# An output projection as seven block products instead of eight

## The chip, the cores and the metric

The kernel runs on one core of a Trainium2 chip. The metric is the time of one execution on the device in microseconds (us), lower is better. A core has TensorE (matmuls into PSUM, called PE in the profile; its weight loads are PEld), VectorE (DVE), ScalarE (ACT), GpSimd (POOL), and SyncE (SP), which here only issues DMAs. PSUM has eight banks of 128 x 512 float32 values; GpSimd does not read it in this kernel.

## What is computed

For 2048 tokens of width 640, with `xn = layernorm(x)`:

```python
# A: linear attention, 32 heads of 20, feature map = two softmaxes
qkv = xn @ wqkv
phi_q, phi_k = features(q, w_phi), features(k, w_phi)
o = (phi_q @ (phi_k.T @ v)) / (phi_q @ sum(phi_k) + 1e-6)
A = o.reshape(S, D) @ wo                  # 2048 x 640 by 640 x 640
# B: an MLP, 640 -> 1728 -> 640
h = gelu(layernorm(xn) @ w1 + b1)
B = h @ w2 + b2
return x + A + B
```

The change concerns the line with `wo`, the output projection.

## The kernel before

Everything is kept transposed: feature chunks of 128 (`KC` = 5 of them) on the partitions, tokens along the free dimension, in four blocks of 512 (`NB` = 4). A float32 operand is split into two parts, a high one (ScalarE copies the value to a shorter type) and a low one (the rest, a subtraction on VectorE or GpSimd; line 57). A product takes three matmuls: high by high, high by low, low by high (`mm3`, line 69).

The stages in order of time: layer norm and the first MLP groups for blocks 0 and 1; from about 217 to 443 us the key stage (the loop at line 1009: keys, queries, values and feature maps for 16 tiles of 128 tokens, four projections to a tile, and `kv_tile`, line 965); then the MLP for blocks 2 and 3 with the attention of all blocks beside it; from 643 us the output projection.

In the key stage only TensorE's order is written by hand; the other engines and the DMA queue are ordered by an automatic scheduler. At its tiles 1, 2, 3, 6 and 7 one chunk of `wo` each is loaded, split, and both parts are stored to DRAM (lines 1035 to 1044). From line 1350 on VectorE, ScalarE and GpSimd too work in program order; the DMAs on SP are still placed by the scheduler.

`Mlp.tick` (line 220) is called after each `mm3`. It counts ticks, runs the steps that are due (`after`, line 227) and advances a generator of side work (`beside`). So a due tick sets at which place of the program an operation enters its engine's queue; the engine runs it when its inputs are there.

MLP groups 1 to 5 for blocks 2 and 3 already use seven block products (`cross`, line 411). For group 6 the two blocks go one after the other (`passes`, line 286).

`Attention` collects a block's result in `ob`. `quotients` (line 1227) divides it by the denominators: five shuffles on VectorE (line 1255) and five multiplications on GpSimd (line 1257). Blocks 0 and 1 are stored to DRAM and come back through `load_ob` (line 1379); those of blocks 2 and 3 stay. The multiplications of block 3 fall into the output projection. `Attention.split` (line 1263) makes a block's two parts, a chunk at a time, while it reorders the tokens: the high part on ScalarE, the low one on VectorE. Then it loads the accumulator (input and MLP sum, `a_dram`) of blocks 0 and 1.

`load_wo` (line 1284) brings the split `wo` back. The projection itself (lines 1400 to 1417) runs over four blocks and five output chunks `m`; for each it sums five contraction chunks in one PSUM bank, with banks 6 and 7 in turn. VectorE adds the bank to the accumulator (line 1416) and SP stores the result (line 1417). The last output chunk is done in two halves of 256 tokens. Splits of blocks 1, 2 and 3 are put at steps 3, 28 and 53.

Of the kernel before, what the change touches and what calls it, by code (L numbers as in the profile page):

```python
# [8 lines left out]
F32 = mybir.dt.float32  # L9
F32R = mybir.dt.float32r  # L10
AF = mybir.ActivationFunctionType
ALU = mybir.AluOpType
# [3 lines left out]
P = 128  # L16
S, D, F, H, DH = 2048, 640, 1728, 32, 20
KC = D // P
NB = S // 512
# [27 lines left out]
def f(ap):  # L47
    return ap.bitcast(F32)
# [3 lines left out]
def tile_kernel(ctx: ExitStack, tc: tile.TileContext, x, xT, wkT, wqT, wv, wphi, wo, w1, b1, w2, b2,  # L52
                ident, mmask, emask, vsel, out):
    nc = tc.nc
    ctx.enter_context(nc.allow_low_precision(reason="float32 operands are split exactly into float32r parts"))

    def split(hi, lo, src, scale=None, eng=nc.vector, first=nc.scalar):

        if scale is None:
            if first is nc.scalar:  # L60
                nc.scalar.activation(hi, src, AF.Copy)  # L61
            else:
                first.tensor_copy(hi, src)
            eng.tensor_tensor(lo, src, f(hi), op=ALU.subtract)  # L64
        else:
            nc.scalar.activation(hi, src, AF.Copy, scale=scale)
            nc.vector.scalar_tensor_tensor(lo, src, scale, f(hi), op0=ALU.mult, op1=ALU.subtract)

    def mm3(ps, lh, ll, rh, rl, first, last, **kw):
        nc.tensor.matmul(ps, lh, rh, start=first, stop=False, **kw)  # L70
        nc.tensor.matmul(ps, lh, rl, start=False, stop=False, **kw)  # L71
        nc.tensor.matmul(ps, ll, rh, start=False, stop=last, **kw)  # L72
# [17 lines left out]
    wo_dram = [tc.dram_tile([P, KC, D], F32, name=f"wo{p}") for p in "hl"]  # L90
# [12 lines left out]
    banks = ctx.enter_context(tc.tile_pool(name="banks", bufs=1, space=PSUM))  # L103
# [110 lines left out]
    class Mlp:  # L214
        def __init__(self, slots, hid):
            self.hid, self.turn, self.slots, self.beside, self.raw = hid, 0, slots, iter(()), {}
            self.ph, self.px, self.po = Banks(0, 1, 2), Banks(3, 4), Banks(5, 6, 7)
            self.due, self.ticks = [], 0

        def tick(self):  # L220

# [5 lines left out]
        def after(self, ticks, step):  # L227

            if ticks:
                self.due.append((self.ticks + ticks, len(self.due) and self.due[-1][1] + 1, step))  # L230
                self.due.sort(key=lambda d: d[:2])
            else:
                step()
# [282 lines left out]
    def finish(p):  # L516
        for _ in p:
            pass
# [4 lines left out]
    x0 = load_x(range(2), xp)  # L523
# [42 lines left out]
    def step(gen, n):  # L566
        for _ in range(n):
            next(gen, None)
# [440 lines left out]
    for t, i in [(t, i) for t in range(14) for i in range(4)] + TAIL:  # L1009
        if (t, i) in ((4, 0), (8, 0)):  # L1010
            b = t // 4 + 1
            y[b] = [yp.tile([P, KC, 512], F32R, name=f"y{p}{b % 2}") for p in range(2)]
            for p in range(2):
                nc.sync.dma_start(f(y[b][p]), y_dram[b - 2][p])
        ps = proj(t, i)
        pq = 1 + t % 3
        if t and t % 4 == 0:
            store_phi(t // 4 - 1, i)
        if i == 0:
            evac = evacuate(ps, 0, 0)  # L1020
# [12 lines left out]
        if tk is not None:  # L1033
            kv_tile(tk, fts.pop(tk), vbuf[tk % 2])
        if i == 0 and t in (1, 2, 3, 6, 7):

            kc = (1, 2, 3, 6, 7).index(t)
            lo = rp.tile([P, D], F32, name="r1")
            hi = rp.tile([P, D], F32R, name="r2")
            nc.sync.dma_start(lo, wo[kc * P:(kc + 1) * P, :])  # L1040
            with tc.issue_after(evac):
                split(hi, lo.bitcast(F32R), lo, eng=nc.gpsimd)
            for w, wd in zip((f(hi), lo), wo_dram):
                nc.sync.dma_start(wd[:, kc, :], w)
        if (t, i) == (11, 0):
            mlp = Mlp((0, 3, 2, 1), ((1, 2), (0, 3)))
            mlp.ph = ptile
            mlp.fetch_pair(0, False)
        if (t, i) == (12, 3):
            with tc.issue_after(evac):  # L1050
                w1t, parts = mlp.take_pair(0, False, 0)
                for part in parts:
                    part()
            mlp.fetch_pair(0, True)
        if (t, i) == (15, 3):
            w2t, late = mlp.take_pair(0, True, 3)
            late.pop(0)()
# [96 lines left out]
    class Attention:  # L1154
# [105 lines left out]
                for i in range(3):  # L1260
                    yield

        def split(self, c, eng):

            b = self.b

            def tokens(ap):
                return ap.rearrange("p (q t n) -> p t q n", q=4, t=4)

            def parts(ap):  # L1270
                return ap.rearrange("p (t q n) -> p t q n", q=4, t=4)

            if c == 0:
                self.oh, self.ol = (yp.tile([P, KC, 512], F32R, name=f"y{p}{b % 2}") for p in range(2))
            if c < KC:
                nc.scalar.activation(parts(self.oh[:, c, :]), tokens(self.ob[:, c, :]), AF.Copy)
            if c:
                eng.tensor_tensor(parts(self.ol[:, c - 1, :]), tokens(self.ob[:, c - 1, :]), f(parts(self.oh[:, c - 1, :])), op=ALU.subtract)
            if c == KC and b < 2:

                acc[b] = tfp.tile([P, KC, 512], F32, name=f"tf{b}")
                nc.sync.dma_start(acc[b], a_dram[b])

    def load_wo():

        for p, wd in enumerate(wo_dram):
            w = wp.tile([P, 4, D], F32R, name=f"w{(2, 0)[p]}")
            nc.sync.dma_start(f(w), wd[:, 0:4, :])
            last = rp.tile([P, D], F32R, name=f"r{1 + p}")
            nc.sync.dma_start(f(last), wd[:, 4, :])  # L1290
            wol.append([w[:, kc, :] for kc in range(4)] + [last])

    def first_split():
        for c in range(KC + 1):
            at[0].split(c, nc.vector)
            if c % 2:
                yield

# [98 lines left out]
    finish(before)  # L1397
    load_ob(1)

    pw_ = Banks(6, 7)  # L1400
    step = 0
    for b in range(NB):
        oh, ol = at[b].oh, at[b].ol
        for m in range(KC):
            ms = slice(m * P, (m + 1) * P)

            for cols in [slice(0, 512)] if (b, m) != (NB - 1, KC - 1) else [slice(0, 256), slice(256, 512)]:
                pw = pw_()[:, cols]
                for c in range(KC):
                    mm3(pw, wol[0][c][:, ms], wol[1][c][:, ms], oh[:, c, cols], ol[:, c, cols], c == 0, c == KC - 1)  # L1410
                    step += 1
                    mlp.tick()
                    for n, at_ in enumerate((3, 28, 53), 1):
                        if step - at_ in range(KC + 1):
                            at[n].split(step - at_, nc.vector)
                nc.vector.tensor_tensor(acc[b][:, m, cols], pw, acc[b][:, m, cols], op=ALU.add)
                nc.sync.dma_start(out[ms, b * 512 + cols.start:b * 512 + cols.stop], acc[b][:, m, cols])
# [63 lines left out]
```

## Time and profile before

| | us |
|---|---|
| median of 3 runs (715.44 to 717.74) | 716.49 |
| the profiled execution | 716.96 |
| its span, first to last instruction | 715.2 |
| PE, DVE, ACT, POOL busy | 704.0, 513.1, 342.1, 421.7 |
| output projection, first matmul to last evacuation | 643.3 to 711.8 |

The profile is one execution. A row of a timeline has the start from the span's beginning, the duration, the engine, the line of the program, the operation and what it writes and reads; in brackets how long the engine was idle before it and what ended that. Several rows of one kind in a row are merged (x2, x3), and then the duration is that of all of them. A row of a table by stretch has the stretch, its length, the busy time and the count of each engine, the granted clock of TensorE, the share of the DMA engines and GB/s. A row of a line's instructions has the shortest, the median and the longest duration in ns.

### The profile page before, as it was taken

Reading aid. Unit: us, or ns where it says so; the run is one execution under the profiler, and the core shown is the slowest. Engines: PE = TensorE matmul, PEld = TensorE weight load, DVE = VectorE, ACT = ScalarE, POOL = GpSimd, SP = SyncE. Lnnn points to the kernel's source line nnn. Section 1 sums busy time; section 2 is a strip of 40 time slices with the busy share of each in tenths; the row PEclk is TensorE's granted clock in tenths of the full one; section 3 lists DMA queues with packets and bytes.
Section 4 is the critical chain, followed back from the end, with each engine's and each line's share of the span. In section 5 each row is a group of like instructions: output and inputs, shape, how many; then the busy total and the mean of one; then the engine's idle time right before and its main releaser. Section 6 shows DMA issues by size and latency. Waiting matters only on the chain.

```text
span 715.2 us, 9745 instructions
## 1 busy us (share of the span) xinstructions
PE 704.0 (98%) x3381; PEld 591.2 (83%) x3381; DVE 513.1 (72%) x820; ACT 342.1 (48%) x563; POOL 421.7 (59%) x360
## 2 busy tenths in 40 slices
PE   8989999999999999999999999999999999999998
PEld 6868888878878888888888888888888878888886
DVE  7776754978754788788888877747679785784632
ACT  6434453444433544554444547357666666560200
POOL 3521223657235998798787979548689887540400
PEclk9999999999999999999999999999999999999999
DMA  9813643474722226325500708864355568545222
GB/s 325 290 44 110 196 134 102 154 243 159 224 91 110 74 91 219 97 89 196 121 0 13 177 0 322 223 205 125 109 160 168 171 181 274 188 127 212 80 83 73
DMA packets 65767, 106.56 MB, mean 149 GB/s; under 512 B 7462, under 2 KB 31814, under 8 KB 63838
## 3 DMA queue, kind: packets, MB, share of 16 engines
q1 hardware_dynamic: 65414, 105.93, 46.5%
q8 instruction: 26, 0.43, 0.2%
q14 instruction: 23, 0.19, 0.1%
q10 hardware_dynamic: 304, 0.01, 0.0%
HBM read 71.37 MB, written 34.55 MB: 148 GB/s over the span
## 4 chain that ended last, share of the span: by engine, by line
PE 79%; DVE 7%; POOL 4%; DMA 4%; issue 3%; ACT 2%; SPq 1%; POOLq 0%; DVEq 0%; ACTq 0%
PE bank L898 23%; PE bank L70 16%; PE bank L72 15%; PE bank L71 15%; PE bank L968 2%; PE bank L696 2%; POOL m L933 2%; PE bank L1206 1%; PE bank L1207 1%; POOL w L64 1%; DMA t<-t 1%; DMA xq<-in_xT 1%; POOL m L944 1%; PE bank L323 1%; PE bank L324 1%
## 5 line engine op out<-in xcount | busy, mean ns | idle before, releaser
L898 PE MATMUL bank<-wkh,y 128*128 128x512 f32 (+1 forms) x480 | 139.5, 364 | 0.0
L70 PE MATMUL bank<-y,w 128*128 128x512 f32 (+1 forms) x294 | 114.4, 389 | 1.0 <-ACT m L283 1.0
L71 PE MATMUL bank<-y,w 128*128 128x512 f32 (+1 forms) x294 | 113.6, 387 | 0.0
L72 PE MATMUL bank<-y,w 128*128 128x512 f32 (+1 forms) x294 | 113.6, 386 | 0.0
L64 POOL TENSOR_TENSOR w<-r,w 128x640 fp32r<-128x640 f32 x32 | 52.2, 1645 | 98.8 <-ACT w L61 68.0
L70 PE MATMUL bank<-m,w 128*128 128x512 f32 x260 | 102.7, 395 | 3.5 <-DVE acc L328 3.2
L72 PE MATMUL bank<-m,w 128*128 128x512 f32 x260 | 101.3, 390 | 0.0
L71 PE MATMUL bank<-m,w 128*128 128x512 f32 x260 | 101.3, 389 | 0.0
L898 PEld LDWEIGHTS bank<-wkh,y 128*128 128x128 f32 x480 | 87.5, 188 | 13.3
L898 PE MATMUL bank<-wkl,y 128*128 128x512 f32 (+1 forms) x240 | 87.4, 364 | 0.0
L70 PEld LDWEIGHTS bank<-y,w 128*128 128x128 f32 x294 | 55.2, 188 | 12.8 <-ACT m L283 1.2
L72 PEld LDWEIGHTS bank<-y,w 128*128 128x128 f32 x294 | 55.2, 188 | 11.3
L71 PEld LDWEIGHTS bank<-y,w 128*128 128x128 f32 x294 | 55.2, 188 | 10.9
L934 ACT ACTIVATE m<-m,rs_all 128x1280 f32<-128x1280 f32 x32 | 43.7, 1365 | 42.9 <-POOL m L933 42.8
L70 PEld LDWEIGHTS bank<-m,w 128*128 128x128 f32 x260 | 48.8, 188 | 15.9 <-DVE acc L328 5.1
L936 DVE TENSOR_REDUCE sm<-m 128x64 f32<-128x1280 f32 x32 | 47.4, 1482 | 15.6 <-ACT m L934 15.4
L898 PE MATMUL bank<-w,y 128*128 128x512 f32 x240 | 57.4, 391 | 0.0
L72 PEld LDWEIGHTS bank<-m,w 128*128 128x128 f32 x260 | 48.8, 188 | 10.3
L71 PEld LDWEIGHTS bank<-m,w 128*128 128x128 f32 x260 | 48.8, 188 | 9.8 <-DVE m L458 0.2
L933 POOL TENSOR_TENSOR m<-m,mx 128x640 f32<-128x640 f32 (+2 forms) x48 | 44.4, 938 | 19.3 <-DVE mx L922 19.3
L328 DVE TENSOR_TENSOR acc<-bank,acc 128x512 f32<-128x512 f32 x70 | 46.9, 684 | 10.5 <-PE bank L72 5.4
L64 DVE TENSOR_TENSOR m<-m,m 128x512 fp32r<-128x512 f32 (+1 forms) x34 | 27.6, 819 | 35.5 <-ACT m L61 35.5
(182 smaller groups left out, 1461.6 us busy)
## 6 DMA issues: line engine op xcount, KB each, us to landing
r<-in_w SPq DMA_DIRECT2D x52, 320.0 KB
e<-e SPq DMA_DIRECT2D x40, 256.0 KB
e<-acc SPq DMA_DIRECT2D x52, 160.0 KB
acc<-in_xT SPq DMA_DIRECT2D x4, 1280.0 KB
t<-t SPq DMA_DIRECT2D x8, 512.0 KB
tf<-t SPq DMA_DIRECT2D x2, 1536.0 KB
xb<-in_x SPq DMA_DIRECT2D x8, 320.0 KB
xq<-in_xT SPq DMA_DIRECT2D x10, 256.0 KB
```

The lines of the kernel that those rows point to most:

```text
L64: eng.tensor_tensor(lo, src, f(hi), op=ALU.subtract)
L70: nc.tensor.matmul(ps, lh, rh, start=first, stop=False, **kw)
L71: nc.tensor.matmul(ps, lh, rl, start=False, stop=False, **kw)
L72: nc.tensor.matmul(ps, ll, rh, start=False, stop=last, **kw)
L323: nc.tensor.matmul(pw, w2h[:, ms], hh, start=False, stop=False)
L328: nc.vector.tensor_tensor(acc[b][:, m, :], pw, acc[b][:, m, :], op=ALU.add)
L696: nc.tensor.matmul(ps[:, u * nh * DF:(u + 1) * nh * DF], raw[:nh * DH, u * P:(u + 1) * P], wpt[:nh * DH, g, :nh, 1:], start=True, stop=True)
L898: nc.tensor.matmul(ps, lh[:, kc, c], rh[:, kc], start=n == 0, stop=n == 3 * KC - 1)
L933: subs[n, t] = nc.gpsimd.tensor_tensor(ep[:, s], a, b, op=ALU.subtract)
L934: exps[n, t] = nc.scalar.activation(e, e, AF.Exp, scale=rs_all[:, t:t + 1])
L936: nc.vector.tensor_reduce(sm, e.rearrange("p s (h f) -> p (s h) f", f=DH), axis=AX, op=ALU.add)
L968: nc.tensor.matmul(kvp[g // 2][:, (g % 2) * 240:(g % 2) * 240 + 240].rearrange("p (s f) -> p s f", s=4), v[:, g * VS:(g + 1) * VS], ft[:, ...
```

## The change

The projection is done by pairs of token blocks (0 and 1, then 2 and 3). For each contraction pair `q` (chunks 2q, 2q+1, of the first four) and each output pair `k` (output chunks 2k, 2k+1, of the first four) the product of two 2 x 2 arrangements of blocks takes seven block products in place of eight, in Winograd's form of Strassen's method. The weight side has the blocks a11, a12, a22 and the sums s1 to s4; the token side has b11, b21, b22 and the differences t1 to t4. Contraction chunk 4 is added by `rest`, output chunk 4 is done as before by `column`.

- In the key stage, at tiles 1 and 6, two chunks of `wo` are loaded, four sums are formed on GpSimd, and chunks and sums (128 x 768) are split and stored. Chunk 4 is done at tile 4.
- `load_wo` has three parts, into other buffers; the accumulators of blocks 0 and 1 go to weight buffers (`load_a`), and `load_ob(1)` is called earlier.
- The differences t1 to t4 are formed in place in `ob` on GpSimd (`combine`, 16 subtractions of 128 x 512) and split like plain blocks (`turn`). All of this is put at written ticks, counted from the projection's start.
- A product's bank is read as soon as its sum is needed and then added to further, so banks 0 to 5 are read several times.
- `after` numbers its steps with a counter of its own; steps due at one tick run in the order in which they were given, as before.

```diff
-        if i == 0 and t in (1, 2, 3, 6, 7):
...
+        if i == 0 and t == 4:
...
+        if i == 0 and t in (1, 6):
+            q = t // 6
+            raw = [rp.tile([P, D], F32, name=f"r{j}") for j in (1, 2)]
...
+            with tc.issue_after(evac):
+                for o, x0, x1, op in ((sm[:, 0], a21, a22, ALU.add), (a21, a11, a21, ALU.subtract),
+                                      (sm[:, 1], sm[:, 0], a11, ALU.subtract), (sm[:, 2], a12, sm[:, 1], ALU.subtract)):
+                    nc.gpsimd.tensor_tensor(o, x0, x1, op=op)
+                o = 0
+                for r, eng in (*zip(raw, 2 * [nc.gpsimd]), (sm.rearrange("p i k n -> p (i k n)"), nc.vector)):
+                    n = r.shape[1]
+                    split(h[:, o:o + n], r.bitcast(F32R), r, eng=eng)
+                    nc.sync.dma_start(wo_dram[1][:, q, o:o + n], r)
+                    o += n
+            nc.sync.dma_start(wo_dram[0][:, q], f(h))
...
+    def load_wo(n):
...
+        else:
+            wop[1][1] = mtile(0, F32R)
+            nc.sync.dma_start(f(wop[1][1]).rearrange("p r d -> p (r d)"), wo_dram[1][:, 1, :1280])
...
+        if b == 3:
+            load_a(0)
...
+            mlp.after(14, lambda: load_wo(0))
         else:
-            load_wo()
+            load_wo(1)
+            load_ob(1)
+            load_wo(2)
             mlp.beside = both(mlp.beside, first_split())
     finish(before)
-    load_ob(1)
+    load_a(1)
...
+    def combine(b0, i, q):
+        c0, c1 = 2 * q, 2 * q + 1
+        (co, bo), (cx, bx), (cy, by) = {1: ((c0, 0), (c0, 1), (c0, 0)), 3: ((c0, 1), (c1, 1), (c0, 1)),
+                                        2: ((c1, 1), (c1, 1), (c0, 0)), 4: ((c1, 0), (c1, 0), (c1, 1))}[i]
+        return lambda: nc.gpsimd.tensor_tensor(at[b0 + bo].ob[:, co], at[b0 + bx].ob[:, cx], at[b0 + by].ob[:, cy], op=ALU.subtract)
...
+    for c in range(KC):
+        steps += both_parts(2 * c, plain, 1, c)
+    for n, i in enumerate((1, 3, 2, 4)):
+        for q in range(2):
+            steps += [(3 + 4 * n + 2 * q, combine(0, i, q)), (38 + 4 * n + 2 * q + 2 * (n > 1), combine(2, i, q))]
+    for n, i in enumerate((1, 2, 4, 3)):
+        for q in range(2):
+            steps += both_parts(11 + 4 * n + 2 * q + (n > 0), turn, 0, i, q)
+            steps += both_parts(47 + 4 * n + 2 * q + 3 * (n > 0), turn, 2, i, q)
+    for n, c in enumerate(range(KC)):
+        steps += both_parts(28 + 2 * c, plain, 2, c)
+    for c, n in ((0, 37), (2, 39), (1, 45), (3, 47), (4, 49)):
+        steps += both_parts(n, plain, 3, c)
+    for tick, step in steps:
+        mlp.after(tick, step)
+
+    for b0 in (0, 2):
+        bank = [{n: banks.tile([P, 512], F32, name=f"bank{3 * k + i}") for i, n in enumerate("abc")} for k in range(2)]
+
+        def read(n, k, i, b, last=True):
+            o = acc[b0 + b][:, 2 * k + i]
+            nc.vector.tensor_tensor(o, bank[k][n], o, op=ALU.add)
...
+        for k in range(2):
+            product("a", k, "a11", "b11", True)
+            read("a", k, 0, 0, False)
+        for k in range(2):
+            product("c", k, "a12", "b21", True)
+            rest("c", k, 0, 0)
+            read("c", k, 0, 0)
+        column(b0, whole)
+        if b0 == 0:
+            column(1, whole)
...
+        for k in range(2):
+            product("a", k, "s3", "t3")
+            read("a", k, 1, 0)
+        for k in range(2):
+            product("b", k, "s4", "b22")
+            rest("b", k, 0, 1)
+            read("b", k, 0, 1)
+        for k in range(2):
+            rest("a", k, 1, 1)
+            read("a", k, 1, 1)
+        if b0 == 2:
+            column(3, halves)
```

`plain` splits a chunk of a block as it is. `both_parts` puts the high part (ScalarE) at the tick and the low part (VectorE) one tick later. The products left out here are s1 by t1 (bank b), s2 by t2 (bank a) and a22 by t4 (bank c, opened anew), in this order after the columns. A `product` has two steps, `q` = 0 and 1.

More of the change, by code (lines that the diff above doesn't have):

```diff
@@ L229, in after @@
             if ticks:
[L230 removed]
+                self.count += 1
+                self.due.append((self.ticks + ticks, self.count, step))
                 self.due.sort(key=lambda d: d[:2])
@@ L1261, in quotients, with split @@
                     yield
[L1263 to L1274, printed above, removed]
+        def split(self, c, part, hl=None):
+            src = self.ob[:, c].rearrange("p (q t n) -> p t q n", q=4, t=4)
+            hi, lo = (z.rearrange("p (t q n) -> p t q n", q=4, t=4) for z in hl or (self.oh[:, c], self.ol[:, c]))
+            if part == 0:
+                nc.scalar.activation(hi, src, AF.Copy)
+            else:
+                nc.vector.tensor_tensor(lo, src, f(hi), op=ALU.subtract)
@@ L1277, in split @@
             if c:
[L1278 to L1291, printed above, removed]
@@ L1293, in first_split @@
-    def first_split():
-        for c in range(KC + 1):
-            at[0].split(c, nc.vector)
+                at[0].split(c - 1, 1)
             if c % 2:
@@ new lines, in tile_kernel, with product, rest, column @@
+    for n, c in enumerate(range(KC)):
[9 more added lines that the diff above has]
+            nc.vector.tensor_tensor(o, bank[k][n], o, op=ALU.add)
+            if last:
+                nc.sync.dma_start(out[(2 * k + i) * P:(2 * k + i + 1) * P, (b0 + b) * 512:(b0 + b + 1) * 512], o)
+        def product(n, k, l, r, start=False):
+            for q in range(2):
+                mm3(bank[k][n], left(l, 0, q, k), left(l, 1, q, k), *right(r, b0, q), start and q == 0, q == 1, skip_group_check=True)
+                mlp.tick()
+        def rest(n, k, i, b):
+            ms = slice((2 * k + i) * P, (2 * k + i + 1) * P)
+            mm3(bank[k][n], wo4[0][:, ms], wo4[1][:, ms], at[b0 + b].oh[:, 4], at[b0 + b].ol[:, 4], False, True, skip_group_check=True)
+            mlp.tick()
+        def column(b, parts):
+            for cols in parts:
+                pw = banks.tile([P, 512], F32, name=f"bank{6 + b % 2 if len(parts) == 1 else 6 + cols.start // 256}")[:, cols]
@@ new lines, in tile_kernel @@
+        for k in range(2):
[6 more added lines that the diff above has]
+        for k in range(2):
+            product("b", k, "s1", "t1", True)
+            read("b", k, 1, 1, False)
+        for k in range(2):
+            product("a", k, "s2", "t2")
+            read("a", k, 0, 1, False)
+        for k in range(2):
+            bank[k]["c"] = banks.tile([P, 512], F32, name=f"bank{3 * k + 2}")
+            product("c", k, "a22", "t4", True)
+            rest("c", k, 1, 0)
+            read("c", k, 1, 0, False)
```

98 lines of the change are left out of this document (76 added, 22 removed).

## The prediction

> **What bounds the kernel now.** I read the head of the page, then the chain that ended last, then what TensorE waited for in the second half, then the busy time by stretch of the output projection.
>
> ```profile
> span 715.2 us, 9745 instructions
> PE 704.0 (98%) x3381; PEld 591.2 (83%) x3381; DVE 513.1 (72%) x820; ACT 342.1 (48%) x563; POOL 421.7 (59%) x360
> PE 79%; DVE 7%; POOL 4%; DMA 4%; issue 3%; ACT 2%; SPq 1%; POOLq 0%; DVEq 0%; ACTq 0%
> ```
> ```profile
> PE bank L70 <- ACT m L283: 1.0, 1, 1.0
> PE bank L1206 <- DVE acc L1220: 0.6, 1, 0.6
> ```
> ```profile
> 643.30:660.30 17.00, 17.00 (x76) 14.10 (x76) 7.57 (x12) 0.00 (x0) 0.00 (x0) 1.00 0.66 228
> 660.30:677.30 17.00, 17.00 (x77) 14.08 (x76) 10.49 (x20) 2.72 (x5) 7.53 (x5) 1.00 0.21 78
> 677.30:694.30 17.00, 17.00 (x77) 14.08 (x76) 6.56 (x10) 2.72 (x5) 0.00 (x0) 1.00 0.21 78
> ```
> TensorE bounds it: busy 98%, in 79% of the chain, and from 445 us on it waited only the two times shown. The columns of the stretches are length, then PE, PEld, DVE, ACT and POOL busy with their counts. Through the projection PE has no gap, ACT and POOL are almost idle, and DVE is never more than 10.5 of 17 us busy. So matmuls taken from the projection shorten the run, as long as nothing that replaces them fills DVE or POOL.
>
> **The change part by part.** I call a group of three matmuls (one mm3, one tick) a step. The scheduled operations are put into each engine's queue in tick order, but run as soon as their data lets them.
>
> *Removed matmuls.* Before: 4 blocks x 5 rows x 5 chunks = 100 steps. After, a pair of blocks takes 7 products x 2 output halves x 2 contraction pairs = 28, plus 8 rest steps for chunk 4 and 10 for output chunk 4: 46, two pairs 92. The halved last column stays. That is 8 steps, 24 matmuls of 512 columns.
>
> ```profile
> 653.80 0.69 DVE L1416 TENSOR_TENSOR tf<-bank,tf 128x512 f32<-128x512 f32 x1 [2.55 <-PE bank L72]
> 657.20 0.69 DVE L1416 TENSOR_TENSOR tf<-bank,tf 128x512 f32<-128x512 f32 x1 [2.71 <-PE bank L72]
> 660.60 0.69 DVE L1416 TENSOR_TENSOR tf<-bank,tf 128x512 f32<-128x512 f32 x1 [2.71 <-PE bank L72]
> 661.22 0.76 DVE L1255 STREAM_SHUFFLE rx<-rx 128x512 f32<-128x512 f32 x1
> 661.84 0.69 DVE L1278 TENSOR_TENSOR y<-acc,y 128x512 fp32r<-128x512 f32 x1
> 662.44 0.77 DVE L1255 STREAM_SHUFFLE rx<-rx 128x512 f32<-128x512 f32 x1
> 663.09 1.15 DVE L1278 TENSOR_TENSOR y<-acc,y 128x512 fp32r<-128x512 f32 x1
> 664.16 0.68 DVE L1416 TENSOR_TENSOR tf<-bank,tf 128x512 f32<-128x512 f32 x1
> 664.76 1.78 DVE L1278 TENSOR_TENSOR y<-acc,y 128x512 fp32r<-128x512 f32 x2
> 666.48 0.72 DVE L1255 STREAM_SHUFFLE rx<-rx 128x512 f32<-128x512 f32 x1
> ```
> (Columns: start, duration, engine and line; waits in brackets.) An evacuation that waits for PE comes every 3.40 us, 15 matmuls: 0.2267 us each, 0.68 us a step. 24 x 0.2267 = **-5.44 us**.
>
> *Added to DVE and POOL.* PSUM is read 37 times instead of 21, and 31 instead of 15 splits fall into the projection. Starts of neighbours (661.22, 661.84, 662.44, 663.09) give 0.60 us for a split or a read and 0.63 for a shuffle. POOL gets 16 subtractions of 128x512; for them I take the multiplications of the same shape.
>
> ```profile
> 662.05 3.34 POOL L1257 TENSOR_TENSOR acc<-acc,rx 128x512 f32<-128x512 f32 x2 [24.30 <-DVE rx L1255]
> 667.28 1.65 POOL L1257 TENSOR_TENSOR acc<-acc,rx 128x512 f32<-128x512 f32 x1 [1.89 <-DVE rx L1255]
> 669.13 2.54 POOL L1257 TENSOR_TENSOR acc<-acc,rx 128x512 f32<-128x512 f32 x2 [0.20 <-DVE rx L1255]
> ```
> Undisturbed, POOL takes 2.54 / 2 = 1.27 us. Beside DVE splits it takes 1.65, and the split that begins at 663.09 in POOL's first operation lasts 1.15 instead of 0.69, the two from 664.76 last 1.78 instead of 1.29: 0.46 and 0.49 us lost. The read at 664.16 and the shuffles between lose nothing. So a split and a POOL operation exclude each other, and a split loses some 0.48 us by it.
>
> The Trainium skill says the same on "SBUF — State Buffer", section "Who interferes with whom": a DVE instruction with two SBUF inputs and a GpSimd instruction reading SBUF fight for one port pair, and the later one fully blocks. The trace agrees (0.46 us above). It speaks against this change, which puts both kinds side by side.
>
> *The seam between the pairs* is where that lands. The second pair's first product reopens bank 0 at step 47, and bank 0 is free only when DVE has read what the rest step of tick 45 left there. Behind what does that read stand? DVE's start in the projection:
>
> ```profile
> 644.30 0.95 DVE L1239 RECIPROCAL dt<-dt 128x128 f32<-128x128 f32 x1
> 645.16 1.23 DVE L1278 TENSOR_TENSOR y<-tf,y 128x512 fp32r<-128x512 f32 x2
> ```
> From 645.16, 1.86 us after the first matmul, up to the read of tick 26 it has 12 splits and 9 reads, 12.6 us; that read waits for its matmuls, 26 x 0.68 + 0.2 = 17.9, and ends at 18.5. From there to the read of tick 45 stand 8 splits (4.8), 5 shuffles of block 3's quotients (3.15) and 8 reads (4.8): 12.75 us, to 31.25. PE comes to step 47 at 46 x 0.68 = 31.28. With no loss at all the read begins when step 45 ends, so PE waits 0.2. But in the same stretch POOL has 9 operations (5 multiplications, 4 subtractions for t1 and t3; 11.4 us), so it is nearly never idle, and I let 7 of the 8 splits meet one: 7 x 0.48 = 3.4. Then PE waits 31.25 + 3.4 - 31.28 = 3.4, and the next bank, one more delayed split later, 0.3: **+3.7 us**. The loss by split lies between 0 and a whole POOL operation, 1.27; I take 0.48, the rows of the very same two instructions. Behind the waiting read stand only DVE's own splits, due 14 steps later or more. Elsewhere each turned block is due at least 7 steps after its split, which covers these losses: nothing.
>
> *Preparing the weights* in the key stage: per half, at tiles 1 and 6, four POOL sums, one more POOL split and a DVE split of 128x768; tiles 2, 3, 7 lose a split each, tile 4 gets one.
>
> ```profile
> L384 POOL TENSOR_TENSOR s<-r x5: 736/744/1188, 450.0 to 570.0; 128x256 f32<-128x256 f32 x5
> L390 POOL TENSOR_TENSOR w<-r,w x20: 1555/1581/2297, 453.8 to 595.7; 128x640 fp32r<-128x640 f32 x20
> L390 DVE TENSOR_TENSOR w<-s,w x5: 1218/2047/2050, 459.0 to 578.7; 128x768 fp32r<-128x768 f32 x5
> ```
> ```profile
> 231.00:245.00 14.00, 14.00 (x69) 11.95 (x68) 11.31 (x18) 7.25 (x12) 12.13 (x12) 1.00 0.21 71
> ```
> ```profile
> 245.57 1.12 PE bank L968 x10
> 246.69 0.08 PE bank L972
> 246.77 12.53 PE bank L898 x60
> ```
> ```profile
> 244.76 0.87 DVE L962 SCALAR_TENSOR_TENSOR v<-bank,rs_all,v 128x480 fp32r<-128x480 f32 x2
> ```
> POOL gets 4 x 0.744 + 1.58 = 4.6 us more in such a tile, and with 12.13 of 14 busy has 1.9 to spare: it falls 2.7 behind and catches up in the two lighter tiles. PE needs the bank read at 244.76 to 245.63 again at 246.77: 1.1 us of cover on the nearest path. DVE, ACT and POOL are placed automatically there, so an evacuation can be put ahead of a late operation. I cost it at nothing; without that cover it is 2 x (4.6 - 1.1) = 7.0, and below nothing there is only the 1.0 us wait on L283.
>
> *Loads.* Only one piece is new and close: the low weights of the second contraction pair, 640 KB, into buffers free after block 2's last matmul, needed at step 2 (644.0).
>
> ```profile
> 637.27 0.39 PE L324 MATMUL bank<-m,w 128*128 128x512 f32 x1
> ```
> ```profile
> 642.62 0.32 SPq L1282 DMA_DIRECT2D tf<-a  x1
> ```
> ```profile
> 648.15 0.69 DVE L1416 TENSOR_TENSOR tf<-bank,tf 128x512 f32<-128x512 f32 x1 [1.76 <-DMA tf<-a]
> ```
> 1280 KB took 5.5 us from issue to use, so 640 KB from 637.7 land by 640.5: nothing. Queued on SP behind a whole 1280 KB load they land at 646.0, 2.0 late. The accumulators move to weight buffers and are loaded earlier, so the DMA wait of 1.76 goes; no PE stood behind it. The end (two half columns, an evacuation, a store) is unchanged.
>
> *Sum against the profiled run* (716.96; 1.76 lie outside its span): -5.44 + 3.7 = -1.74, 715.22. The median of the runs is 0.47 lower: **714.7**.
>
> **The rivals.**
>
> *No wait at the seam.* The splits and POOL miss each other, or the queue runs ahead. For it: DVE's own work just fits (31.25 against 31.28). Against it: three rows of mutual delay in five POOL operations. 716.49 - 5.44 + 0.2 = 711.3.
>
> *Slower: every split waits out a whole POOL operation.* One mechanism, at the seam: POOL has always the next operation ready, so a split loses 1.27, 7 x 1.27 = 8.9, PE waits 9.2: 716.49 - 5.44 + 9.2 = 720.3. It eats the gain from 0.7 us a split on, and is measurably slower from 1.0 on. For it: the 768-column split above lost 2.047 - 1.218 = 0.83. Against it: DVE's reads and shuffles take no part, so POOL slips through beside them.
>
> *The key stage stalls.* POOL is 87% busy there, and its lag reaches PE: +7.0 on the forecast, 721.7. Against it: before, PE has no gap there at all with a split in five tiles.
>
> *The clock drops at the seam.* A wait in one piece of over 3 us may let TensorE's clock fall.
>
> ```profile
> 713.00:714.00 1.00, 0.00 (x0) 0.00 (x0) 0.00 (x0) 0.00 (x0) 0.00 (x0) 1.00 0.39 131
> 714.00:715.20 1.20, 0.00 (x0) 0.00 (x0) 0.00 (x0) 0.00 (x0) 0.00 (x0) 0.57 0.00 0
> ```
> ```profile
> 1.31 5.72 PE L575 MATMUL bank<-m 128*128 128x512 f32 x18 [1.31 <-POOL m L573]
> ```
> After the last matmul (711.8) the granted clock stays 1.00 for over 2 us, then falls to 0.57. The first 18 matmuls of the run took 5.72 instead of 4.08 us, so a cold start costs 1.6: 714.7 + 1.6 = 716.3. On "TensorE: Matmul & The Clock Gate", section "Why this matters for your kernels", the Trainium skill asks for no idle gap above some 3 us; the fall at 714 agrees.
>
> That the change does not do what it says can't be: the steps are counted from the loops.
>
> **How the numbers follow.** Forecast 0.50, with 712.8 (0.2 us a split) to 717.2 (0.83) as its own range; no wait 0.22; clock 0.08; whole-operation wait 0.10; key stage 0.10. A measurement of this kernel tells about 0.3%, 2.15 us, from no change: below 714.3 is faster, above 718.6 slower. The forecast straddles 714.3: I give 0.22 of its 0.50 to faster. Faster 0.22 + 0.22 = 0.44; same 0.28 + 0.08 = 0.36; slower 0.20. The range leaves out the two slow rivals: from 711.0, a little below the no-wait case, to 718.5, the forecast with a late load and the clock.
>
> **What would show it.** Right: 24 fewer matmuls at 0.2267; one PE wait of 2 to 5 us some 31 us after the projection's start, released by a DVE read, with splits of 1.0 us and more before it beside POOL subtractions. Wrong: no such wait (711), PE waits between 230 and 320 us, a wait for a weight load at step 2, or PE waits for turned blocks inside a pair.

## The result, and the profile after

| | before | after |
|---|---|---|
| median of 4 runs each, same chip (us) | 716.59 (715.44 to 717.74) | 724.84 (722.89 to 726.02) |
| ratio, 95% interval | | 1.0112 (1.0084 to 1.0140) |
| the profiled execution, its span (us) | 716.96, 715.2 | 724.43, 722.6 |
| projection: first matmul to the start of the last evacuation (us) | 643.30 to 711.79, 68.49 long | 648.21 to 719.06, 70.85 long |

The change makes the kernel slower by some 8 us, where 714.7 was forecast. The head of the page and the chain, as for before:

```profile
span 722.6 us, 9806 instructions
PE 704.7 (98%) x3357; PEld 590.5 (82%) x3357; DVE 549.3 (76%) x854; ACT 353.1 (49%) x581; POOL 453.9 (63%) x384
PE 73%; DVE 11%; POOL 7%; issue 4%; DMA 2%; ACT 1%; SPq 0%; DVEq 0%; POOLq 0%; ACTq 0%
```
TensorE has its 24 matmuls less (3357 against 3381) and yet is busy as long as before: a part of them ran slower. Its share of the chain fell from 79 to 73%, and VectorE's and GpSimd's rose from 11 to 18%. What TensorE waited for (lines of the table of waits: total, times, longest):

```profile
PE bank L70 <- DVE w L1505: 4.8, 3, 3.0
PE bank L900 <- DVE v L964: 2.5, 2, 2.3
PE bank L70 <- ACT m L285: 1.4, 1, 1.4
```
The first is the seam (L1505 is the read of a bank in the projection). The second is new and lies in the key stage: the key projection (L900) waits for the evacuation L964. The third was 1.0 before. Busy time by stretch of the projection (length, PE, PEld, DVE, ACT, POOL, granted clock, DMA share, GB/s):

```profile
648.21:665.21 17.00, 17.00 (x76) 14.09 (x75) 17.00 (x21) 3.44 (x7) 9.71 (x6) 1.00 0.42 149
665.21:678.21 13.00, 13.00 (x58) 10.52 (x56) 13.00 (x23) 4.65 (x9) 5.77 (x4) 1.00 0.05 20
678.21:690.21 12.00, 7.16 (x20) 4.92 (x20) 12.00 (x16) 3.15 (x5) 9.32 (x8) 0.72 0.36 132
690.21:707.21 17.00, 17.00 (x77) 14.06 (x76) 12.32 (x17) 2.94 (x5) 3.92 (x3) 1.00 0.13 47
```
VectorE is full from the first matmul to the end of the seam, not only at the seam, and in the third stretch the granted clock is 0.72.

**Where the time went.** The projection starts 4.91 us later and takes 2.36 us more; with 5.44 us of matmuls gone, something in it costs 7.8 us.

*Before the projection.* The ten matmuls of `kv_tile` (L968 before, L970 after) come every 13.73 us in both traces. Between the sixth and the seventh tile of after they come 17.77 us apart (313.31 to 331.08): 4.04 us lost in one tile. Before the last tiles another 1.2 us go (13.12 in place of 12.49, and smaller pieces). That is 5.2; the first `kv_tile` of after comes 0.75 us earlier than that of before, and the third wait above is 0.4 longer, which leaves the 4.9. Timeline rows of after around the loss, GpSimd, ScalarE, VectorE and TensorE:

```profile
307.80 2.52 POOL L935 TENSOR_TENSOR m<-m,mx 128x640 f32<-128x640 f32 x1
...
311.59 1.37 ACT L936 ACTIVATE m<-m,rs_all 128x1280 f32<-128x1280 f32 x1 [3.49 <-POOL m L935]
...
312.99 1.49 DVE L938 TENSOR_REDUCE sm<-m 128x64 f32<-128x1280 f32 x1 [2.08 <-ACT m L936]
...
316.00 0.84 DVE L964 SCALAR_TENSOR_TENSOR v<-bank,rs_all,v 128x480 fp32r<-128x480 f32 x2
...
316.98 0.76 PE L900 MATMUL bank<-wkh,y 128*128 128x512 f32 x1 [2.31 <-DVE v L964]
```
Read from the bottom: TensorE waits 2.31 us for the evacuation that begins at 316.00. That stands in VectorE's queue behind four transposes and a sum (L938), which waits for ScalarE (L936), which waits for GpSimd (L935). GpSimd is late by its added sums and splits, and this L935, which begins while VectorE is in a split (L64, 307.65 to 309.11), takes 2.52 us where the next of the same shape takes 1.27. After the wait the matmuls come 0.43 us apart, twice the usual distance, until 320.46: eight in 3.48 us in place of 1.81, 1.67 us lost. 2.31 + 1.67 is nearly all of the tile's 4.04.

*At the seam.* VectorE's and GpSimd's rows of after:

```profile
658.03 2.88 DVE L1291 TENSOR_TENSOR m<-tf,m 128x512 fp32r<-128x512 f32 x2
662.53 1.77 DVE L1291 TENSOR_TENSOR e<-tf,e 128x512 fp32r<-128x512 f32 x1
667.83 0.68 DVE L1505 TENSOR_TENSOR w<-bank,w 128x512 f32<-128x512 f32 x1
675.77 1.44 DVE L1291 TENSOR_TENSOR y<-acc,y 128x512 fp32r<-128x512 f32 x1
678.38 3.46 DVE L1291 TENSOR_TENSOR y<-acc,y 128x512 fp32r<-128x512 f32 x2
681.76 0.68 DVE L1505 TENSOR_TENSOR w<-bank,w 128x512 f32<-128x512 f32 x1
683.73 1.87 DVE L1505 TENSOR_TENSOR w<-bank,w 128x512 f32<-128x512 f32 x3
```
```profile
656.92 6.84 POOL L1464 TENSOR_TENSOR tf<-tf,tf 128x512 f32<-128x512 f32 x4
679.58 1.71 POOL L1464 TENSOR_TENSOR acc<-acc,acc 128x512 f32<-128x512 f32 x1
```
```profile
682.49 0.79 PE L70 MATMUL bank<-y,r 128*128 128x512 f32 x1 [3.01 <-DVE w L1505]
...
685.75 0.77 PE L70 MATMUL bank<-y,w 128*128 128x512 f32 x1 [1.61 <-DVE w L1505]
...
689.17 0.40 PE L72 MATMUL bank<-y,w 128*128 128x512 f32 x1
```
The read at 667.83 is that of tick 26. It ends at 668.43; on time it would end 18.5 us after the start, at 666.7. So VectorE comes 1.7 us late into the stretch: the splits of the first pair beside the four subtractions of 6.84 us take up to 1.77. (The twelve splits before that read lose 4.4 us in all, and 2.7 of it was room. The prediction had counted more room: in after a reciprocal, at 653.12, stands inside this list, which before ran ahead of it.) From 668.43 to the end of the read of tick 45 (the last of the three from 683.73, 685.53) pass 17.1 us, where the list is worth 12.75: 4.35 lost, in eight splits. VectorE is never idle meanwhile, so it does not wait for GpSimd's results: its own instructions get longer.

The longest wait, 3.01 us, is not that of the second pair's first product but comes one step earlier. The matmul at 682.49 is step 46, the last rest step of the first pair; it adds to a bank whose read (tick 38, at 681.76) stands behind the two splits of 3.46 us. The matmul at 685.75 is step 47, the second pair's first product, which waits another 1.61 for the read of tick 45: it comes 37.54 us after the start in place of 31.28, 6.26 late. Then eight matmuls at the slow distance (685.75 to 689.17) take 3.42 in place of 1.81 us: 1.6. Together 7.9, the seam's cost.

### The profile page after: what moved, and what is told of

Same layout as the page of the kernel before. It is cut to its first block, busy times and chain, and to the rows that moved or that the text cites. A ratio compares the mean times of both kernels' runs of the same rounds, so it can differ in the third digit from the quotient of the medians.

```text
span 722.6 us, 9806 instructions
## 1 busy us (share of the span) xinstructions
PE 704.7 (98%) x3357; PEld 590.5 (82%) x3357; DVE 549.3 (76%) x854; ACT 353.1 (49%) x581; POOL 453.9 (63%) x384
## 4 chain that ended last, share of the span: by engine, by line
PE 73%; DVE 11%; POOL 7%; issue 4%; DMA 2%; ACT 1%; SPq 0%; DVEq 0%; POOLq 0%; ACTq 0%
PE bank L900 20%; PE bank L70 15%; PE bank L72 14%; PE bank L71 14%; POOL m L935 3%; PE bank L698 2%; DVE y L1291 1%; POOL m L946 1%; PE bank L970 1%; PE bank L1227 1%; PE bank L1228 1%; DVE w L1505 1%; DVE acc L330 1%; POOL w L64 1%; DVE rx L1276 1%
## 5 line engine op out<-in xcount | busy, mean ns | idle before, releaser
L900 PE MATMUL bank<-wkh,y 128*128 128x512 f32 (+1 forms) x480 | 140.9, 367 | 2.9 <-DVE v L964 2.5
L64 POOL TENSOR_TENSOR w<-r,w 128x640 fp32r<-128x640 f32 x32 | 52.2, 1644 | 99.1 <-ACT w L61 68.2
L70 PE MATMUL bank<-m,w 128*128 128x512 f32 x280 | 110.7, 395 | 2.8 <-DVE acc L330 2.5
L71 PE MATMUL bank<-m,w 128*128 128x512 f32 x280 | 109.1, 390 | 0.0
L72 PE MATMUL bank<-m,w 128*128 128x512 f32 x264 | 102.9, 390 | 0.0
L70 PE MATMUL bank<-y,w 128*128 128x512 f32 (+1 forms) x254 | 99.8, 393 | 3.0 <-DVE w L1505 1.6
L900 PEld LDWEIGHTS bank<-wkh,y 128*128 128x128 f32 x480 | 88.3, 190 | 16.8 <-issue 2.4
L71 PE MATMUL bank<-y,w 128*128 128x512 f32 (+1 forms) x254 | 98.7, 389 | 0.0
L72 PE MATMUL bank<-y,w 128*128 128x512 f32 (+1 forms) x228 | 88.7, 389 | 0.0
L900 PE MATMUL bank<-wkl,y 128*128 128x512 f32 (+1 forms) x240 | 88.0, 366 | 0.0
L70 PEld LDWEIGHTS bank<-m,w 128*128 128x128 f32 x280 | 52.6, 188 | 16.2 <-DVE acc L330 4.8
L938 DVE TENSOR_REDUCE sm<-m 128x64 f32<-128x1280 f32 x32 | 47.4, 1480 | 19.3 <-ACT m L936 19.2
L71 PEld LDWEIGHTS bank<-m,w 128*128 128x128 f32 x280 | 52.6, 188 | 10.5 <-DVE m L460 0.2
L935 POOL TENSOR_TENSOR m<-m,mx 128x640 f32<-128x640 f32 (+2 forms) x48 | 45.6, 965 | 21.9 <-DVE mx L924 21.9
L70 PEld LDWEIGHTS bank<-y,w 128*128 128x128 f32 x254 | 48.2, 190 | 13.7 <-ACT y L1289 2.3
L936 ACT ACTIVATE m<-m,rs_all 128x1280 f32<-128x1280 f32 x32 | 43.6, 1362 | 31.8 <-POOL m L935 31.6
L72 PEld LDWEIGHTS bank<-m,w 128*128 128x128 f32 x264 | 49.6, 188 | 10.4
L900 PE MATMUL bank<-w,y 128*128 128x512 f32 x240 | 57.4, 391 | 0.0
L71 PEld LDWEIGHTS bank<-y,w 128*128 128x128 f32 x254 | 48.2, 190 | 9.5
L64 DVE TENSOR_TENSOR m<-m,m 128x512 fp32r<-128x512 f32 (+1 forms) x34 | 27.4, 814 | 35.0 <-ACT m L61 34.9
L900 PEld LDWEIGHTS bank<-w,y 128*128 128x128 f32 x240 | 44.4, 188 | 8.5
```

The source lines that it names most:

```text
L900: nc.tensor.matmul(ps, lh[:, kc, c], rh[:, kc], start=n == 0, stop=n == 3 * KC - 1)
L935: subs[n, t] = nc.gpsimd.tensor_tensor(ep[:, s], a, b, op=ALU.subtract)
L936: exps[n, t] = nc.scalar.activation(e, e, AF.Exp, scale=rs_all[:, t:t + 1])
L938: nc.vector.tensor_reduce(sm, e.rearrange("p s (h f) -> p (s h) f", f=DH), axis=AX, op=ALU.add)
```

## The experiments

The theory after this: two losses that have nothing to do with each other, one from the weight preparation in the key stage, one at the seam, each a wait made longer by a fall of TensorE's clock. Its rivals: the loss is all in the projection (or all before it), or VectorE simply has too many instructions and GpSimd is beside the point. Medians of before beside these kernels are 716.34 us for the first seven and 716.72 for the last two.

**One half at a time: key_only and proj_only.** key_only is before with the new preparation (and the old projection); proj_only is after with the old preparation. Their edits:

```diff
# key_only, against before
-        if i == 0 and t in (1, 2, 3, 6, 7):
+        if i == 0 and t == 4:
...
+        if i == 0 and t in (1, 6):
# proj_only, against after
-        if i == 0 and t == 4:
...
-        if i == 0 and t in (1, 6):
...
+        if i == 0 and t in (1, 2, 3, 6, 7):
```


> The kernel before with the new preparation of wo in the key stage; the old projection then reads these arrays, so the block a21 of its weights holds a11 - a21. Theory: the GpSimd burst at tile 6 makes TensorE wait 2.3 us and run some 20 matmuls at half clock, 4.0 us, and the later part of the stage gives up nearly 1 us more: 716.6 + 4.9 = 721.5. Rival (the loss in that stage belongs to the new loads or to the projection's other needs): 716.6.

> The new projection with the old preparation, one chunk of wo split at each of five tiles; the sums of weight blocks are not formed, pieces of the chunks stand in their place. Theory (two separate losses): 724.8 less the 4.9 of the key stage, 719.9, with the same waits of 4.8 us at the seam and the slow matmuls behind them. Rival (the seam is late because the key stage upset the order or the loads): no wait at the seam, 711.5.

Measured: key_only 720.52 us, ratio 1.0074 (1.0047 to 1.0102); proj_only 719.36 us, 1.0045 (1.0029 to 1.0062). +4.2 and +3.0, in sum 7.2 of 8.3: two losses, and they add up to within 1.1 us. In key_only the tile took 15.84 us and the wait was this:

```profile
PE bank L899 <- DVE v L963: 2.2, 2, 1.9
```
In proj_only no tile is late, and the seam is that of after to the digit:

```profile
PE bank L70 <- DVE w L1491: 4.8, 3, 3.0
```

**Who makes VectorE late at the seam: no_combine and no_pool.** The first leaves out the second pair's eight subtractions on GpSimd, the second all GpSimd work of the projection.

```diff
# no_combine
-            steps += [(3 + 4 * n + 2 * q, combine(0, i, q)), (38 + 4 * n + 2 * q + 2 * (n > 1), combine(2, i, q))]
+            steps += [(3 + 4 * n + 2 * q, combine(0, i, q)), (38 + 4 * n + 2 * q + 2 * (n > 1), lambda: None)]
# no_pool: the same for combine(0, i, q) too, and
-                    nc.gpsimd.tensor_tensor(ob[:, c - 1, :], ob[:, c - 1, :], rx[:, c - 1, :], op=ALU.mult)
+                    if self.b < 3:
+                        nc.gpsimd.tensor_tensor(ob[:, c - 1, :], ob[:, c - 1, :], rx[:, c - 1, :], op=ALU.mult)
```


> The changed kernel without the eight GpSimd subtractions of the second pair (its t blocks are split as they are); VectorE's list is the same. Theory (VectorE's own work just fills the stretch, and port exclusion with GpSimd makes it late): waits at the seam fall from 4.8 to about 2.5 us, what is left coming from five multiplications and VectorE's own list, and the clock does not drop: 724.8 - 2.3 - 2.2 = 720.3. Rival A (VectorE has too much work, GpSimd plays no part): waits stay at 4.8, 724.8. Rival B (exclusion with the subtractions alone): waits of 0.3 us, 717.6.

> After without any GpSimd work in the projection: the 16 subtractions that form t1 to t4 and block 3's five multiplications by the quotients are left out, so block differences and block 3's values are not formed; every matmul, VectorE operation and ScalarE split stays. Theory (VectorE's list up to the read of tick 45 just fits by itself, 31.25 us against 31.28, and the whole delay of step 47 is time lost to GpSimd: 1.7 us by which the read of tick 26 is late after the first pair's subtractions, plus 4.4 us lost by the eight splits behind it): with nothing on GpSimd the waits for VectorE at the seam go from 4.8 us to below 0.5, the granted clock stays at 1.00 there, and the time is the projection's full gain with the key stage's loss left: 716.4 + 4.2 - 5.4 + 0.2 = 715.4 us. Rival (VectorE has simply too many instructions in that stretch, GpSimd is beside the point): waits of 3 us and more stay, the clock falls as before, and the time is 722 to 724 us.

Measured: no_combine 723.84 us, ratio 1.0105 (1.0073 to 1.0138), waits of 3.9 us in place of 4.8, and the clock falls all the same, for thirteen matmuls instead of eleven (the three of step 46 and the eight behind them). So the second pair's subtractions are only the smaller part, and the expectation (2.5) was wrong. no_pool 716.48 us, 0.9995 (0.9983 to 1.0007), with this one wait at the seam, and these stretches beside it:

```profile
PE bank L70 <- DVE w L1506: 0.2, 1, 0.2
```
```profile
660.00:675.00 15.00, 15.00 (x68) 12.43 (x67) 13.29 (x26) 1.68 (x3) 0.00 (x0) 1.00 0.10 35
675.00:690.00 15.00, 14.80 (x66) 11.97 (x65) 13.24 (x23) 5.95 (x11) 0.00 (x0) 1.00 0.39 141
```
VectorE has the same list and now 1.7 us to spare in each 15. The projection takes 63.41 us (648.18 to 711.59), 5.08 less than before. So the list fits, the matmuls taken out are worth what was said, and all of the seam's loss comes from GpSimd beside VectorE. (The median is 1.1 us above the expectation, not for the seam: this trace's projection starts 4.9 us later than that of before, as in after, where 4.2 was reckoned.) no_combine shows how it is made up. There the read of tick 26 ends 20.2 us after the start, as late as in after, since the first pair's subtractions remain; from there to the read of tick 45 it is 15.5 us: 2.75 lost beside block 3's multiplications alone, against 4.35. So of the 6.1 us by which GpSimd makes VectorE late in after, 1.7 come from the first pair's subtractions, 2.75 from the multiplications, which were there before the change, and 1.6 from the second pair's subtractions.

The Trainium skill, "SBUF — State Buffer", section "Who interferes with whom", calls the port pair that VectorE and GpSimd share an exclusive lock; no_pool agrees, 4.8 us of waits against 0.2 with the same VectorE work.

**Room at the seam: seam.** In the second pair the column of output chunk 4, which needs neither banks 0 to 5 nor turned blocks, goes first, and block 3's plain splits and the second pair's subtractions go to other ticks.

```diff
-    for c, n in ((0, 37), (2, 39), (1, 45), (3, 47), (4, 49)):
+    for c, n in ((0, 42), (2, 46), (1, 49), (3, 53), (4, 76)):
...
+        if b0 == 2:
+            column(2, whole)
         for k in range(2):
             product("a", k, "a11", "b11", True)
...
-        column(b0, whole)
         if b0 == 0:
+            column(0, whole)
```


> The changed kernel with all its work; the plain column of block 2 is put at the start of the second pair, five steps that need neither bank 0 nor bank 3, and the splits of block 3 and the subtractions of the second pair enter their queues later. Theory: the reads have 3.4 us more, so waits of under 1 us and no fall of the clock: 724.8 - 7.3 = 717.5. Rival (the waits belong to the total work of VectorE, not to its order): they move to a later product, 723 to 725.

Measured: 718.76 us, ratio 1.0032 (1.0015 to 1.0049). The waits at the seam are 1.2 us in sum, both before the last two rest steps of the first pair, the longest 1.0 at step 46; no matmul there is slow, and the projection takes 64.95 us (647.72 to 712.67). In the key stage the tile still took 17.31 us. It is 1.3 us above the expectation: against after the projection won 5.9 us, where 7.3 was expected, and 1.2 us of waits are left in it.

**The burst in the key stage: spread, both, late, both2.** The new preparation is, in one tile, four sums and two splits on GpSimd and one split on VectorE. spread moves the parts to several tiles; both is seam and spread together; late is seam with the second burst whole at tile 9; both2 is seam with the parts spread and the rows loaded a tile ahead of their use.

```diff
# spread and both, against after and seam
-        if i == 0 and t == 4:
+        if i == 0 and t == 5:
-        if i == 0 and t in (1, 6):
+        if i == 0 and t in (1, 7):
...
+        if i == 0 and t in (2, 3, 4, 8, 9, 10):
+            o, r, eng = wsrc.pop(0)
# late, against seam
-        if i == 0 and t in (1, 6):
+        if i == 0 and t in (1, 9):
# both2: as spread, but chunk 4 at t == 4, the loads at t in (1, 6), the sums at t in (1, 7)
```


> After with the new weight preparation spread over more tiles: sums at tiles 1 and 7, the three splits of each half at tiles 2, 3, 4 and 8, 9, 10, chunk 4 at tile 5. The amount of work is the same. Theory (the burst of four sums and two splits in one tile keeps GpSimd busy for 14.00 of 14 us and makes the evacuation late): the 2.3 us wait before tile 7's key projections goes, every kv tile comes 13.7 us after the one before up to tile 12, the key stage gives back its 4.2 us, and the time is 724.8 - 4.2 = 720.6 us; at least 722 if only half of it goes. Rival (the sum of the added work is what counts, wherever it stands): tiles get later by the same amount in all, and the time stays at 724 to 725 us.

> The reordered seam (column of output chunk 4 first in the second pair, block 3's plain splits and the second pair's subtractions at other ticks) together with the spread weight preparation. Theory (the two losses are separate, the seam's and the key stage's, and add up): seam alone was 718.76, less the key stage's 3.6 us there: 715.2 us or less; with nothing lost at all it would be 716.4 - 5.4 = 711.0, and some 1.2 us of waits at the seam and 0.4 us at the key stage's end stay: 712.6 us. So 712.5 to 715.5 us, and faster than before. Rival (spreading moves the loss elsewhere): 718 to 719 us, slower than before.

> The reordered seam with the whole burst of the second half (two loads, four sums, three splits) at tile 9 in place of tile 6, where the DMA engines are idle and GpSimd has 10.7 of 14 us of its own work a tile. Theory A (the burst itself decides: 4 sums and 2 splits are 6.1 us, and GpSimd has 3.3 us to spare in a tile): one tile near the tenth is late by 3 to 4 us, and the time is that of seam, 718.8 us. Theory B (the place decides, because GpSimd was behind at tile 6 after chunk 4 and the feature stores): no tile is late, and the time is 718.8 - 3.6 = 715.2 us or less.

> The reordered seam with the weight preparation spread out in another way: in spread and both GpSimd's first sum of the second half stood 4.3 us in its queue for the load of the weight rows, which was issued at 296.3 us behind chunk 4's stores and sixteen stores of features. Here chunk 4 stays at tile 4, the rows of the second half are loaded at tile 6 and used from tile 7 on; sums at tiles 1 and 7, splits at tiles 2, 3, 4 and 8, 9, 10. Theory (lateness in the key stage comes from GpSimd falling behind by a burst, or by a load in its queue, with VectorE's evacuation queued behind work that waits for GpSimd): no kv tile is late any more, the key stage takes what it took before, 1.2 us of waits stay at the seam, and the time is 716.4 - 5.4 + 1.2 + 0.5 = 712.7 us, at most 714. Rival (the sum of the added work makes tiles late wherever it stands): 3 to 4 us lost in the key stage as in seam and spread, 717 to 719 us.

spread measured 724.42 us, 1.0111 (1.0095 to 1.0126): nothing won. It says little on the burst, because a new wait took its place. GpSimd's first sum and SP's issues in spread:

```profile
300.81 0.73 POOL L1058 TENSOR_TENSOR s<-r,r 128x256 f32<-128x256 f32 x1 [4.33 <-DMA r<-in_wo]
```
```profile
280.66 11.71 SPq L1003 DMA_DIRECT2D e<-acc  x16
293.10 0.98 SPq L1045 DMA_DIRECT2D wo4l<-r  x1
296.30 1.17 SPq L1051 DMA_DIRECT2D r<-in_wo  x2
```
The rows of the second half go into the buffers that chunk 4 is stored from, so their load was issued only behind those stores, and these stood behind sixteen feature stores. GpSimd, in order, stood 4.33 us before its sum, and everything that waits for it with it. both has nearly the same wait (4.14 us): 717.69 us, 1.0024 (1.0013 to 1.0035). Its expectation, 712.5 to 715.5, was missed.

late measured 718.35 us, 1.0019 (1.0005 to 1.0032). The loss moved with the burst: tiles six and seven are 13.73 us apart, and the late one (15.68) is at 354.5 to 370.2. Its rows, on GpSimd, ScalarE, VectorE and TensorE, are those of after, and so are the waits, but for TensorE's, 1.78 us in place of 2.31:

```profile
348.48 2.53 POOL L935 TENSOR_TENSOR m<-m,mx 128x640 f32<-128x640 f32 x1
...
352.28 1.37 ACT L936 ACTIVATE m<-m,rs_all 128x1280 f32<-128x1280 f32 x1 [3.50 <-POOL m L935]
...
353.68 1.49 DVE L938 TENSOR_REDUCE sm<-m 128x64 f32<-128x1280 f32 x1 [2.08 <-ACT m L936]
...
356.69 0.83 DVE L964 SCALAR_TENSOR_TENSOR v<-bank,rs_all,v 128x480 fp32r<-128x480 f32 x2
...
357.67 0.47 PE L900 MATMUL bank<-wkh,y 128*128 128x512 f32 x1 [1.78 <-DVE v L964]
```
The first of its two theories had the form right, and neither the size: the burst costs 2.0 us at tile 9 as at tile 6, and the rest of what seam loses in that tile, 1.6, is the clock, which did not fall in this trace. The median is still only 0.4 us below seam's, because in most executions of late the clock did fall somewhere: in six of the ten the mean granted clock is 0.998 or less, and they took 718.32 to 719.91 us, the four others 715.77 to 717.65. In seam it is four of five (718.01 to 719.87 against 716.69). Besides, TensorE waits 0.9 us more in late's MLP stage (L71 for L460). The burst at tile 1, for which the first `kv_tile` is not yet there, costs nothing in any run.

both2 measured **714.75 us** against 716.72, ratio **0.9973** (0.9964 to 0.9982): faster than before and than after. Its page and its waits:

```profile
span 713.6 us, 9801 instructions
```
```profile
PE bank L70 <- DVE w L1509: 1.2, 2, 1.0
PE bank L70 <- ACT m L285: 1.0, 1, 1.0
PE bank L900 <- DVE v L964: 0.9, 1, 0.9
```
The projection takes 64.93 us, 3.56 less than before, and starts 1.94 later. In none of its eleven executions is the mean granted clock below 0.999. The expectation was 712.7, at most 714, and what is missing lies in three places: the key stage ends 1.1 us later than before, where 0.5 was counted (one tile still takes 14.79 us and another 13.98, and GpSimd still waits 1.55 us for the rows); the MLP stage behind it takes 0.8 more, in small pieces; and the projection wins 0.7 less than its waits explain. The cause of the last two is open. The loss of 1.2 us in the last tiles, which every kernel with the burst has, is down to 0.1; why spreading the burst removes it no run shows.

## Why the prediction was wrong

It named the two places and most of the mechanism, and put the sign wrong: two of its terms were too small, and two of its rivals, taken as exclusive, came true together and on top of the forecast. Against the profiled run: -5.44 + 7.9 at the seam + 4.9 before the projection = 7.4; measured 724.43 - 716.96 = 7.47.

- **Removed matmuls, -5.44:** right. no_pool's projection is 5.08 us shorter with 0.2 of wait.
- **The key stage at nothing:** this is the first step that failed. "An evacuation can be put ahead of a late operation" was a hope about the scheduler with no row behind it. The rows show the evacuation behind the sum L938 in VectorE's queue, and that behind GpSimd through ScalarE. It was priced as a rival at 7.0 with a chance of 0.10. That rival's form (GpSimd's lag reaches TensorE) was right. Its size was made up otherwise: one burst of two, 2.3 us of wait, 1.67 of slow clock, and about 1.2 in the last tiles. The backlog of 2.7 us and the cover of 1.1 were both written down, and their difference, 1.6, is near the waits of 1.8 to 2.3 that came; the forecast did not use it.
- **The seam at +3.7:** right in the releaser and the mechanism, too small by half. That VectorE's list fits by itself was right (no_pool), though the reciprocal was left out of it. The step that failed is the start: the read of tick 26 was taken as on time, because the loss per split was charged only behind it. The first pair's splits meet four subtractions of GpSimd as well, and that read ends 1.7 us late. The loss of the eight splits was 4.35 us, 0.54 each, against 7 x 0.48 = 3.4. The place was a step off: only the read of tick 45 was looked at, but most of the wait, 3.01 of 4.8 us, stood before step 46, which needs the read of tick 38.
- **The clock:** named as a rival at +1.6 for a wait of "over 3 us". The price came out at the seam, 1.6, in part by luck: the clock was low there for 6.8 us, and for 1.9 of them TensorE stood idle anyway. The condition was wrong (and the 0.57 of its row is a mean: in that trace the clock is 0.50 from 714.18 us on). The fall came a second time, for 1.67 us in the key stage, after a wait of 2.31.
- **Loads at nothing, turned blocks at nothing, the end unchanged:** right; the table of waits of after has no such line.
- **Its own signs:** the wait at the seam and the long splits were seen, and so was the sign against it, waits of TensorE between 230 and 320 us.

## What to carry to other kernels

Fewer matmuls paid only when the work that replaces them was laid out by the queue of every other engine; the same arithmetic gave 724.8 us in one order and 714.75 in another. When an added operation is called free, find what stands behind it in its queue and on whom the next evacuation of PSUM waits in its own queue: here it was four engines long. Where one cause (GpSimd beside VectorE) acts in several stretches, charge it in each, the one before the tight place too, and add up rivals that can happen together. Look at every step that needs a bank again, not only at the one that opens it anew.

## What the hardware showed that was not expected

How long a wait lets TensorE's clock fall. The rows below are, in this order, two of seam, one of key_only and one of late, each around the wait for the key stage's evacuation: 1.81, 1.92 and 1.78 us long (PE's busy time is the second figure, the granted clock the third from the end):

```profile
313.75:317.16 3.41, 1.60 (x11) 1.34 (x11) 3.38 (x10) 1.62 (x2) 2.04 (x5) 1.00 0.00 0
317.16:320.57 3.41, 3.41 (x10) 2.64 (x9) 1.81 (x3) 1.27 (x1) 3.41 (x4) 0.50 0.00 0
```
```profile
314.37:317.79 3.42, 1.87 (x8) 1.59 (x9) 3.39 (x7) 1.37 (x1) 2.05 (x3) 1.00 0.00 0
```
```profile
356.42:359.83 3.41, 2.16 (x10) 1.81 (x11) 3.34 (x7) 1.36 (x1) 2.05 (x3) 1.00 0.33 101
```
1.81 us was enough in seam, and 1.92 was not in key_only (nor 1.78 in late), so the length of the wait does not decide alone. What does is in the traces, which record every change of the granted clock. In all eleven, each change lies a whole number of stretches of 3.413 us after the first rise: in after the clock stays at 1.00 for 91 of them, at 0.50 for one, at 1.00 for 106, at 0.50 for two. When the run is cut at these edges, the clock falls at the end of a stretch in which TensorE was idle for 1.81 us or more, and at no other: the most idle stretch that kept the clock had 1.76 (at 38.34 us of before). The wait of seam lies in one stretch as a whole. That of key_only is cut by the edge at 314.37, with 1.55 us behind it, and that of late by the edge at 356.42, with 1.25. A low stretch with 0.99 us of idle time or more was followed by another low one, and one with 0.36 or less by the full clock. So the slow time was 3.41 us in the key stage and 6.83 at the seam of after, where 1.77 us of idle time fall into the first low stretch. (The ends of matmuls are modelled by the profiler, so the idle times are good to some hundredths of a microsecond at best.)

The edges have no fixed place: the first comes 4.2 to 7.2 us after the start of these traces, and executions of one kernel differ in whether the clock fell (late, above). So nearly the same wait can cost 1.6 us in one execution and nothing in another.

On "TensorE: Matmul & The Clock Gate", section "What's actually happening", the Trainium skill describes a free-running window of 3413 ns by which activity is judged; the edges agree with it, 3.413 us apart and at another place in each trace. The Trainium skill asks on the same page, in "Why this matters for your kernels", for no gap above some 3 us; here 1.81 within one window was enough, and the measurement decides.
